# Retention and feed-forward in one kernel: outputs of two chunks in two PSUM banks, first up projections paired, first down projections by rows of w_out, first block's results evicted by ScalarE

## The chip, the cores and the metric

The kernel runs on one core of a Trainium2 chip. The metric is the device time of one execution in microseconds (us); the kernel before has a median of 309.3 us over 3 runs (308.94 to 309.8). Times inside an execution are counted from the start of the profiled span.

The engines are named as the profile names them: PE (TensorE, matrix multiplication; PEld is its weight load), DVE (VectorE), ACT (ScalarE), POOL (GpSimd) and SP (SyncE, which here only issues transfers). Each engine works through its own queue in order; engines wait for each other through semaphores.

## The reference

Eight batches, eight heads, 576 positions, head size 64. A retention layer without softmax feeds a two-layer feed-forward block with a gated activation:

```python
scores = scale * np.matmul(q, k.transpose(0, 1, 3, 2))
gamma = 1.0 - 2.0 ** (-5.0 - np.arange(H))
rel = pos[:, None] - pos[None, :]
Dmat = np.where(rel >= 0, gamma[:, None, None] ** rel[None, :, :], 0.0)
attn = np.matmul(scores * Dmat, v)
x = attn.transpose(0, 2, 1, 3).reshape(B * S, H * D)   # 4608 x 512
h = x @ w_in                                           # 512 -> 2048
g = h * (1.0 / (1.0 + np.exp(-beta * h)))
return g @ w_out                                       # 2048 -> 512
```

All inputs and the output are float32. The kernel multiplies in bfloat16.

## The kernel before, in words

**Blocks and chunks.** The first 512 positions of each batch are one block of 512 rows. The last 64 positions of all eight batches together are a ninth block. A block's attention is worked in four chunks of 128 keys. Index `i` counts chunks over all blocks in the order of `seq`: 0 to 3 are block 0, 4 to 7 block 1, 8 to 11 block 2.

**One chunk.** `pre` casts keys (`kn`) and scales values (`vn`) on POOL. `t_k` transposes the keys on PE into a PSUM tile `T`, and another engine copies it to `kT` (from block 2 on, a DMA transposes instead: `x_q`, `x_k`). `a_sc` makes the scores of all heads in two PSUM tiles, and DVE multiplies them by the causal mask into `R`. `a_cross` adds to the output tile `O` what earlier chunks contribute, from the state `sbd`; `a_O` adds the chunk's own part. `a_x` evicts `O` into `xT`, the transposed input of the feed-forward. `a_st` updates the state in PSUM, and ACT copies it to `sbd` (after a block's last chunk to `end`).

**Feed-forward.** `up(m, fo)` multiplies block `m`'s `xT` by 128 columns of w_in, four matmuls over `ko`; ACT applies the activation into `gT`. `down(m, ms, f0)` multiplies four rows `fo` of `gT` for a 128-row slice `ms` by four row groups of w_out; after the last of sixteen rows the slice is evicted from `po` to `ot` and stored. Block 1's first ten ups run in halves (256 columns), so that they can begin with chunks 4 and 5 alone.

**Weights.** w_in and w_out are loaded once, in float32, through a tile `wt` with four buffers, and cast to bfloat16 in SBUF: w_in in pieces of 256 or 512 columns by `cast_w_in`, w_out in four groups of four row groups by `cast_w_out`, which also divides by beta. Before the change w_in has four pieces of 256 and two of 512 columns, one transfer each. In the 256-column pieces DVE casts `ko` 0 and 1 and POOL 2 and 3; in the larger ones POOL casts only `ko` 3. ACT casts the last row group of each group of w_out.

**PSUM.** Eight banks: the tag `mm` has three (ups, downs, some transposes and scores), `O` two, `sc` two, `st` one. A tile takes a buffer of its tag when the buffer's last reader in program order is done.

**Order.** It is written out by hand. Block 0's attention is a straight list of calls with small matmuls between (`warm_up`), followed by `cast_w_in(0)` and `(1)`. From then on PE follows one list, `fill`: the ups of block 0 (16 entries), its downs (`d0` is their first index, 16 entries), the ups of block 1 (`u1`), and so on. All other work hangs on positions in that list: each entry of `streams` is a pair of a position and a call, and `merged` emits a call just before the first fill entry whose index is at least its position. So `(d0 + 10.6, t_q)` is emitted before fill entry `d0 + 11`. All transfers but one go through the queue of SP, in the order of emission, and move on the same sixteen DMA engines.

Of the kernel before, what the change touches and what calls it, by code (L numbers as in the profile page):

```python
# [19 lines left out]
def kernel(  # L20
# [127 lines left out]
    causal4 = consts.tile([P, HP, P], BF16, name="causal4")  # L148
    nc.gpsimd.tensor_copy(causal4[:], causal[:].unsqueeze(1).to_broadcast([P, HP, P]))

# [16 lines left out]
    pieces = [(f, 256) for f in range(0, 1024, 256)] + [(f, 512) for f in range(1024, d_ff, 512)]  # L167
# [5 lines left out]
    def load_w_in(g):  # L173
        f0, fn = pieces[g]
        if f0 % 512 == 0:
            whole[0] = stage.tile([P, KO, 512], F32, name="wt", tag="wt", bufs=4)
        t = whole[0][:, :, f0 % 512:f0 % 512 + fn]
        nc.sync.dma_start(t, w_in_r[:, :, f0:f0 + fn])  # L178
        wts[g] = t

    def cast_w_in(g, kos=range(KO)):
        t = wts[g]
        f0, fn = pieces[g]
        for ko in kos:
            on_pool = ko == KO - 1 or g < 4 and ko > 1
            (nc.gpsimd if on_pool else nc.vector).tensor_copy(w_in_sb[:, ko, f0:f0 + fn], t[:, ko])  # L186
# [6 lines left out]
    def cast_w_out(g):  # L193
        t = wts.pop(NP + g)
        for i in range(KO):
            fo = g * KO + i
            if i == KO - 1:
                nc.scalar.activation(w_out_sb[:, fo, :], t[:, i], ACT.Copy, scale=rbeta_sb[:, fo:fo + 1])
            else:
                nc.vector.tensor_scalar(w_out_sb[:, fo, :], t[:, i], rbeta_sb[:, fo:fo + 1], None, ALU.mult)  # L200
# [99 lines left out]
    def t_k(i):  # L300
        T = psum.tile([P, HP, P], BF16, name="T", tag="sc" if i in (CB + 2, CB + 3) else "O", bufs=2)
        for p in range(HP):
            nc.tensor.transpose(T[:, p, :], heads(live[i]["kn"], p), ident[:])
        nc.scalar.copy(live[i]["kT"], T[:])  # L304
# [8 lines left out]
    def a_sc(i):  # L313
        L = live[i]
        L["R"] = R = sb.tile([P, 2, HP, P], BF16, name="R", tag="R", bufs=4)

        tag = "mm" if i == CB - 1 else "O" if i >= E and (i - E) % 2 else "sc"
        sc = [psum.tile([P, HP, P], F32, name="sc", tag=tag, bufs=3 if tag == "mm" else 2) for _ in range(2)]
        for p in range(HP):
            for j in range(2):  # L320
                r = slice(j * D, (j + 1) * D)
                rhs, view = q_cols(i, r, p)
                nc.tensor.matmul(view(sc[j][:, p, :]), L["kT"][r, p, :], rhs, start=True, stop=True,  # L323
                                 skip_group_check=True)
        mask = causal if seq[i][0] is not None else causal2
        m_b = mask[:].unsqueeze(1).to_broadcast([P, HP, P])
        if i == CB - 1:

            half = sb.tile([P, HP, P], BF16, name="half", tag="half", bufs=1)
            nc.scalar.copy(half[:], sc[1][:])  # L330
            sc[1] = half
        for j in range(2):
            nc.vector.tensor_tensor(R[:, j], sc[j][:], causal4[:] if i == CB - 1 else m_b, ALU.mult)  # L333

    def a_cross(i, first):

        b, c = seq[i]
        L = live[i]
        if first:
            L["O"] = psum.tile([P, HP, P], F32, name="O", tag="O", bufs=2)  # L340
        if c == 0 and b is not None:
            return
        for p in range(HP):
            rhs, view = q_cols(i, slice(0, P), p)
            if b is None:
                for x in range(2):
                    r = slice(x * TL, (x + 1) * TL)
                    nc.tensor.matmul(L["O"][:, p, r], ends[(2 * c + x) % 4][:, p, :], rhs[:, r],  # L348
                                     start=False, stop=True, skip_group_check=True)
            else:  # L350
                nc.tensor.matmul(view(L["O"][:, p, :]), sbds[(c - 1) % NS][:, p, :], rhs,  # L351
                                 start=first and p == 0, stop=not first, skip_group_check=True)

    def a_O(i):
# [5 lines left out]
        if not early:  # L360
            tag = "sc" if b is not None and b >= QB and c > 1 else "O"
            L["O"] = psum.tile([P, HP, P], F32, name="O", tag=tag, bufs=2)
        O, R, vn = L["O"], L["R"], L["vn"]
        crossed = b is None or c > 0
        for j, p in [(n // HP, n % HP) if early else (n % 2, n // 2) for n in range(H)]:
            nc.tensor.matmul(O[j * D:(j + 1) * D, p, :], vn[:, 2 * p + j, :], R[:, j, p, :],  # L366
                             start=p == 0 and not (early and crossed), stop=early or not crossed,
                             skip_group_check=True)
        if early:
            a_x(i)  # L370

    def a_x(i):
        b, c = seq[i]
        O = live[i]["O"]
        if b is None:
            x = xt(B)[:, :, c, :]
        else:
            x, O = xt(b)[:, :, :, c * PC:(c + 1) * PC], O.rearrange("k p (i s) -> k p i s", i=CB)
        if i == CB - 1:
            nc.vector.tensor_copy(x[:, :2], O[:, :2])  # L380
            nc.scalar.copy(x[:, 2:], O[:, 2:])
        else:
            on_act = i < E or i % 2 == 0 if i < 2 * E else b is not None and c == 1
            (nc.scalar.copy if on_act else nc.vector.tensor_copy)(x, O[:])  # L384
# [31 lines left out]

    pos_, ots, held = {}, {}, []
# [5 lines left out]
    def down(m, ms, f0, fn=4, n0=0, nn=d_model):  # L423
# [13 lines left out]
        nc.vector.tensor_copy(ot, po[:, :nn])  # L437
# [43 lines left out]
    a_O(0)  # L481
    a_sc(1)
# [7 lines left out]
    t_k(3)  # L490
    warm_up(1, 128)
    a_cross(2, True)
    a_sc(3)
    pre(2, (1,))
    a_st(2)
    a_O(2)
    pre(3, (1,))
    warm_up(2, 128)
    a_cross(3, True)
    a_O(3)  # L500
    cast_w_in(0)
# [9 lines left out]
    fill = [F(up, 0, fo) for fo in range(FO)]  # L511
    d0 = len(fill)
    fill += [F(down, 0, ms, f0) for f0 in range(0, FO, 4) for ms in range(3)]
# [14 lines left out]
    def second(i):  # L528
        for f in (a_O, lambda j: a_cross(j, False), a_x):
# [4 lines left out]
    streams = [[(0, F(load_w_out, 0)), (1.1, F(cast_w_in, 2)), (3.1, F(cast_w_in, 3)), (3.2, F(load_w_out, 1)),  # L534
                (6.1, F(cast_w_in, 4)), (6.2, F(load_w_out, 2)), (10.1, F(cast_w_in, 5)), (10.2, F(load_w_out, 3))],
# [6 lines left out]
               [(d0 + 7, F(pre_q, 1, n)) for n in range(4)] + [(d0 + 12.5, F(pre_q, XB, n)) for n in range(4)] + [(d0 + 10.6, F(t_q, 1, 0)), (d0 + 12.6, F(t_q, 1, 1))],  # L542
               [(d0 + 8, F(pre, 4, (0,))), (d0 + 8, F(pre, 5, (0,))), (d0 + 9, F(pre, 4, (1,))), (d0 + 9, F(pre, 5, (1,))),
                (d0 + 12.7, F(t_k, 4)), (d0 + 12.8, F(t_k, 5)), (d0 + 13.8, F(a_sc, 4)), (d0 + 13.81, F(a_sc, 5)),
                (d0 + 14.8, F(a_st, 4)), (d0 + 15.9, F(second, 4))],
               [(d0 + 10, F(pre, 6, (0,))), (d0 + 10, F(pre, 7, (0,))), (d0 + 12, F(pre, 6, (1,))), (d0 + 12, F(pre, 7, (1,))),
                (d0 + 15.8, F(t_k, 6)), (d0 + 15.91, F(t_k, 7)), (u1 + 1.8, F(a_sc, 6)), (u1 + 1.81, F(a_sc, 7)),
                (u1 + 2.8, F(a_st, 6)), (u1 + 8.8, F(second, 6))]]
# [32 lines left out]
    for n in range(1, B - 1):  # L581
# [3 lines left out]
        lo, hi = (base[n] + 16, base[n + 1] - 9.5) if n == 1 else (base[n] + 3, base[n + 1] - 8)  # L585
# [44 lines left out]
```

## Time and profile before

The profiled execution took 309.26 us, of which 307.6 us are the span of the program's instructions. The rest of this text counts in that execution.

| what | us |
|---|---|
| median of 3 runs | 309.3 |
| profiled execution | 309.26 |
| its span | 307.6 |
| PE busy in the span | 297.1 (97%) |
| PE idle | about 10.5 |
| first up of block 0 starts | 19.08 |
| first down of block 0 starts | 34.00 |
| first up of block 1 starts | 52.10 |
| last matmul ends | 303.9 |

The feed-forward's matmuls are most of it: the page gives the up projections (line 413) 128.2 us of PE and the down projections (line 430) 126.5. The transfers are busy early: until 40 us the queue moves 211 to 388 GB/s, and its sixteen engines show busy shares around 1.0 in every stretch. Group lines read as: line, engine, operation, output from inputs with their sizes, count, then busy time and the mean of one. Timeline lines read as: start, length, engine, line, operation, count, and in brackets the engine's idle time before it with what ended that.

### The profile page before, as it was taken

The numbers are of one execution on the slowest core, as the hardware profiler recorded it, in microseconds if no ns is written. First come the engines' busy times: TensorE is split into PE (matmuls) and PEld (weight loads), VectorE is DVE, ScalarE is ACT, GpSimd is POOL, SyncE is SP. The second block draws the span as 40 slices with busy tenths as digits, with TensorE's granted clock in tenths as the row PEclk, the third lists the DMA queues.
The fourth block names the chain that finished last, engine by engine and source line by source line (L and its number), as shares of the span: only waits on it lengthen the run. The fifth ranks groups of instructions, "written<-read, shape, count | busy, mean of one in ns | idle before, by whom it ended". The sixth has DMA issues, their size and how long they took to land.

```text
span 307.6 us, 5289 instructions
## 1 busy us (share of the span) xinstructions
PE 297.1 (97%) x2112; PEld 156.5 (51%) x2145; DVE 106.0 (34%) x190; ACT 141.6 (46%) x251; POOL 96.6 (31%) x131
## 2 busy tenths in 40 slices
PE   8889999999999999999999999999999999999995
PEld 6543456755554454454554545454545544444444
DVE  7554476304730433234430623052424520020012
ACT  5666626882248313660286208710772048107600
POOL 4753016836433392181326030912330000000000
PEclk9999999999999999999999999999999999999999
DMA  8999999999999999997994499939980110121012
GB/s 210 221 357 387 380 238 265 209 187 275 182 268 237 244 219 227 251 169 158 196 245 86 105 226 241 181 90 206 200 125 16 76 49 0 33 69 36 0 68 70
DMA packets 128120, 53.84 MB, mean 175 GB/s; under 512 B 109904, under 2 KB 120544, under 8 KB 128096
## 3 DMA queue, kind: packets, MB, share of 16 engines
q1 hardware_dynamic: 128064, 53.49, 78.3%
q8 instruction: 17, 0.28, 0.4%
q14 instruction: 7, 0.06, 0.1%
q10 hardware_dynamic: 32, 0.01, 0.0%
HBM read 36.71 MB, written 9.44 MB: 150 GB/s over the span
## 4 chain that ended last, share of the span: by engine, by line
PE 88%; SPq 4%; DMA 4%; issue 1%; DVE 1%; ACT 0%
PE po L430 40%; PE ph L413 38%; DMA wt<-in_moe_w_in_dram 4%; SPq L94 3%; PE sc L323 3%; PE O L366 3%; PE st L396 2%; PE O L351 2%; SPq L178 1%; DVE xT L384 0%; DVE w_in_sb L186 0%; PE O L348 0%; SPq L81 0%; PE T L297 0%; ACT sbd L401 0%
## 5 line engine op out<-in xcount | busy, mean ns | idle before, releaser
L415 ACT ACTIVATE gT<-ph,beta_sb 128x512 bf16<-128x512 f32 (+1 forms) x154 | 100.2, 660 | 83.0 <-PE ph L413 82.6
L413 PE MATMUL ph<-xT,w_in_sb 128*128 128x512 bf16 (+1 forms) x600 | 128.2, 365 | 2.6 <-DVE w_in_sb L186 0.9
L430 PE MATMUL po<-w_out_sb,gT 128*128 128x512 bf16 (+2 forms) x591 | 126.5, 368 | 1.0 <-issue 0.3
L413 PEld LDWEIGHTS <-w_in_sb 128*128 128x128 bf16 x616 | 58.9, 98 | 64.8 <-DVE w_in_sb L186 2.5
L430 PEld LDWEIGHTS <-gT 128*128 128x128 bf16 x608 | 57.1, 98 | 62.6
L333 DVE TENSOR_TENSOR R<-sc,causal 128x512 bf16<-128x512 f32 x71 | 44.3, 684 | 78.3 <-PE sc L323 78.3
L437 DVE COPY ot<-po 128x512 f32<-128x512 f32 (+2 forms) x38 | 25.0, 662 | 85.9 <-PE po L430 85.8
L255 POOL TENSOR_TENSOR vn<-kvn,gv 128x512 bf16<-128x512 f32 x32 | 33.3, 1044 | 17.8 <-DMA kvn<-in_v_dram 9.1
L273 POOL CAST kn<-kvn 128x512 bf16<-128x512 f32 x32 | 19.6, 613 | 52.4 <-DMA kvn<-in_k_dram 51.9
L247 POOL TENSOR_TENSOR qs<-qn,gq 128x512 bf16<-128x512 f32 x24 | 24.3, 1043 | 26.4 <-DMA qn<-in_q_dram 26.4
L401 ACT CAST sbd<-st 64x256 bf16<-64x256 f32 x48 | 17.4, 363 | 18.6 <-PE st L396 18.0
L384 DVE CAST xT<-O 128x512 bf16<-128x512 f32 x24 | 15.8, 688 | 18.7 <-PE O L366 9.1
L384 ACT CAST xT<-O 128x512 bf16<-128x512 f32 x11 | 6.5, 587 | 31.4 <-PE O L351 31.2
L396 PE MATMUL st<-vn,kn 128*128 128x128 bf16 x128 | 12.4, 219 | 0.1
L396 PEld LDWEIGHTS <-kn 128*128 128x128 bf16 x128 | 9.2, 98 | 4.8
L366 PE MATMUL O<-R,vn 128*64 128x128 bf16 x288 | 11.2, 221 | 0.1
L366 PEld LDWEIGHTS <-vn 128*64 128x64 bf16 x288 | 8.8, 109 | 4.3 <-issue 3.8
L323 PE MATMUL sc<-qT,kT 64*128 64x128 bf16 x256 | 10.3, 217 | 0.3 <-ACT kT L304 0.2
L262 POOL TENSOR_TENSOR kn<-tln,gq 128x512 bf16<-128x512 f32 x4 | 4.2, 1044 | 18.9 <-DMA tln<-in_q_dram 13.6
L323 PEld LDWEIGHTS <-kT 64*128 64x128 bf16 x288 | 8.1, 94 | 3.6 <-ACT kT L304 1.1
L208 PE MATMUL ph<-warm 128*128 128x128 f32 (+1 forms) x24 | 7.3, 444 | 1.2 <-DVE warm L119 1.2
L186 DVE CAST w_in_sb<-wt 128x256 bf16<-128x256 f32 (+1 forms) x14 | 5.8, 464 | 5.5 <-DMA wt<-in_moe_w_in_dram 5.4
(56 smaller groups left out, 84.8 us busy)
## 6 DMA issues: line engine op xcount, KB each, us to landing
qn<-in_q_dram SPq DMA_DIRECT2D x16, 512.0 KB, 5.7
kvn<-in_k_dram SPq DMA_DIRECT2D x32, 256.0 KB, 4.8
kvn<-in_v_dram SPq DMA_DIRECT2D x32, 256.0 KB, 5.1
out_dram<-ot SPq DMA_DIRECT2D x31, 256.0 KB, 3.1
wt<-in_moe_w_out_dram SPq DMA_DIRECT2D x4, 1024.0 KB, 9.5
wt<-in_moe_w_in_dram SPq DMA_DIRECT2D x4, 512.0 KB, 7.5
wt<-in_moe_w_in_dram SPq DMA_DIRECT2D x2, 1024.0 KB, 11.9
out_dram<-ot SPq DMA_DIRECT2D x9, 128.0 KB, 2.4
```

Source lines behind the costliest of these rows:

```text
L247: e.tensor_tensor(batch[b]["qs"][:, cs, hs], q_tiles[b][:, hs, cs].rearrange("p h i d -> p i h d"), gq[:, cs, hs].unsqueeze(3).to_broadcas ...
L255: nc.gpsimd.tensor_tensor(live[i]["vn"][:], kv_tiles.pop(i)[:, 1], gains(gv, c), ALU.mult)
L273: nc.gpsimd.tensor_copy(kn[:, c % 2], t[:, 0])
L323: nc.tensor.matmul(view(sc[j][:, p, :]), L["kT"][r, p, :], rhs, start=True, stop=True, skip_group_check=True)
L333: nc.vector.tensor_tensor(R[:, j], sc[j][:], causal4[:] if i == CB - 1 else m_b, ALU.mult)
L366: nc.tensor.matmul(O[j * D:(j + 1) * D, p, :], vn[:, 2 * p + j, :], R[:, j, p, :], start=p == 0 and not (early and crossed), stop=early or ...
L384: (nc.scalar.copy if on_act else nc.vector.tensor_copy)(x, O[:])
L396: nc.tensor.matmul(st[:, p, :], heads(L["kn"], p), heads(L["vn"], p), start=(c == 0 and p == 0), stop=True, skip_group_check=True)
L413: nc.tensor.matmul(ph, w_in_sb[:, ko, fo * P:(fo + 1) * P], xts[m][:, ko, :, w], start=(ko == 0), stop=(ko == KO - 1))
L415: nc.scalar.activation(gts[m][:, fo, :, w], ph, ACT.Silu, scale=beta_sb[:, fo:fo + 1])
L430: nc.tensor.matmul(po[:, :nn], gT[:, fo, ms, :], w_out_sb[:, fo, n0:n0 + nn], start=(fo == 0), stop=(fo == FO - 1))
L437: nc.vector.tensor_copy(ot, po[:, :nn])
```

## The change

Its parts, in the order of the program:

1. The mask copy `causal4` is gone; the scores of chunk 3 are masked by DVE straight from both PSUM tiles, without the copy `half` by ACT.
2. w_in has six pieces of 256 columns and one of 512. The first two and the last are loaded in two transfers each (`ko` 0, 1 and `ko` 2, 3). POOL casts `ko` 0 and 1 of piece 0, and `ko` 1 and 3 of the others; the 512-column piece is cast for `ko` 2 and 3 in halves of 256 columns.
3. POOL instead of ACT casts the last row group of w_out's first group.
4. The output tiles of chunks 3 and 5 are split over two PSUM buffers (`split`, `new_O`, `O_of`, `opens`); DVE evicts one, ACT the other.
5. `a_x` is called by itself in the front, for chunk 1 after `t_k(3)`; `a_sc(3)` goes ahead of `a_cross(2)`.
6. Evictions: in block 1 ACT takes chunk 4 whole and half of chunk 5, DVE the rest; DVE copies `kT` of chunks 6 and 7; ACT evicts block 0's downs.
7. The first two ups of block 0 are paired: `ko` 0 and 1 of both, then `ko` 2 and 3 of both. The first twelve down matmuls go row group by row group over three slices.
8. Positions: block 1's and block 2's attention steps are shifted among the fill entries.

```diff
-    causal4 = consts.tile([P, HP, P], BF16, name="causal4")
-    nc.gpsimd.tensor_copy(causal4[:], causal[:].unsqueeze(1).to_broadcast([P, HP, P]))
...
-    pieces = [(f, 256) for f in range(0, 1024, 256)] + [(f, 512) for f in range(1024, d_ff, 512)]
+    pieces = [(f, 256) for f in range(0, 1536, 256)] + [(f, 512) for f in range(1536, d_ff, 512)]
...
-        nc.sync.dma_start(t, w_in_r[:, :, f0:f0 + fn])
+        for w in (slice(0, 2), slice(2, KO)) if g in (0, 1, NP - 1) else (slice(0, KO),):
+            nc.sync.dma_start(t[:, w], w_in_r[:, w, f0:f0 + fn])
...
-            on_pool = ko == KO - 1 or g < 4 and ko > 1
-            (nc.gpsimd if on_pool else nc.vector).tensor_copy(w_in_sb[:, ko, f0:f0 + fn], t[:, ko])
+            on_pool = ko < 2 if g == 0 else ko % 2
+            e = nc.gpsimd if on_pool else nc.vector
+            if fn > 256 and ko == 2:
+                for x in range(0, fn, 256):
+                    for o, eng in ((2, nc.vector), (3, nc.gpsimd)):
+                        eng.tensor_copy(w_in_sb[:, o, f0 + x:f0 + x + 256], t[:, o, x:x + 256])
+            elif fn == 256 or ko < 2:
+                e.tensor_copy(w_in_sb[:, ko, f0:f0 + fn], t[:, ko])
...
-            if i == KO - 1:
+            if i == KO - 1 and g == 0:
+                nc.gpsimd.tensor_tensor(w_out_sb[:, fo, :], t[:, i], rbeta_sb[:, fo:fo + 1].to_broadcast([P, d_model]), ALU.mult)
+            elif i == KO - 1:
...
-        nc.scalar.copy(live[i]["kT"], T[:])
+        (nc.vector.tensor_copy if i in (CB + 2, CB + 3) else nc.scalar.copy)(live[i]["kT"], T[:])
...
-        if i == CB - 1:
-
-            half = sb.tile([P, HP, P], BF16, name="half", tag="half", bufs=1)
-            nc.scalar.copy(half[:], sc[1][:])
-            sc[1] = half
...
+    def split(i):
+        return i in (CB - 1, CB + 1)
+
+    def new_O(i):
+        b, c = seq[i]
+        if split(i):
+            tags = ("sc", "sc") if i == CB - 1 else ("O", "sc")
+            live[i]["O"] = [psum.tile([P, 2, P], F32, name="O", tag=t, bufs=2) for t in tags]
+        else:
+            tag = "sc" if b is not None and b >= QB and c > 1 else "O"
+            live[i]["O"] = [psum.tile([P, HP, P], F32, name="O", tag=tag, bufs=2)]
...
-        if i == CB - 1:
-            nc.vector.tensor_copy(x[:, :2], O[:, :2])
-            nc.scalar.copy(x[:, 2:], O[:, 2:])
+        if split(i):
+            nc.vector.tensor_copy(x[:, :2], view(Os[0]))
+            nc.scalar.copy(x[:, 2:], view(Os[1]))
         else:
-            on_act = i < E or i % 2 == 0 if i < 2 * E else b is not None and c == 1
+            on_act = i < E + 2 or i >= 2 * E and b is not None and c == 1
...
+    def up_pair(m, fo, u):
...
+        fs = (fo, fo + 1)
+        if u == 0:
+            for f in fs:
+                phs[f] = psum.tile([P, MB], F32, name="ph", tag="mm", bufs=3)
+        for f, ko in [(f, ko) for ko in (0, 1) for f in fs] if u == 0 else [(f, ko) for f in fs for ko in (2, 3)]:
+            nc.tensor.matmul(phs[f][:], w_in_sb[:, ko, f * P:(f + 1) * P], xts[m][:, ko],
+                             start=(ko == 0), stop=(ko == KO - 1))
+            if ko == KO - 1:
+                nc.scalar.activation(gts[m][:, f], phs[f][:], ACT.Silu, scale=beta_sb[:, f:f + 1])
...
-        nc.vector.tensor_copy(ot, po[:, :nn])
+        (nc.scalar.copy if m == 0 else nc.vector.tensor_copy)(ot, po[:, :nn])
...
-    a_cross(2, True)
-    a_sc(3)
+    a_x(1)
+    warm_up(1, 128)
+    a_sc(3)
+    a_cross(2, True)
...
-    fill = [F(up, 0, fo) for fo in range(FO)]
+    fill = [F(up_pair, 0, fo, u) for fo in (0,) for u in range(2)] + [F(up, 0, fo) for fo in range(2, FO)]
     d0 = len(fill)
-    fill += [F(down, 0, ms, f0) for f0 in range(0, FO, 4) for ms in range(3)]
+    def down_rows(n):
+
+        for x in range(4 * n, 4 * n + 4):
+            down(0, x % 3, x // 3, 1)
+
+    fill += [F(down_rows, n) for n in range(3)]
+    fill += [F(down, 0, ms, f0) for f0 in range(4, FO, 4) for ms in range(3)]
     fill += [F(down, 0, 3, f0) for f0 in range(0, FO, 4)]
```

The positions that change, by call (others stay):

| call | before | after |
|---|---|---|
| `t_q(1, 0)` | d0 + 10.6 | d0 + 11.6 |
| `t_k(5)` | d0 + 12.8 | d0 + 14 |
| `a_sc(4)`, `a_sc(5)` | d0 + 13.8, 13.81 | d0 + 14, 15 |
| `a_st(4)` | d0 + 14.8 | d0 + 15 |
| `t_k(6)`, `t_k(7)` | d0 + 15.8, 15.91 | d0 + 15.95, u1 + 1 |
| `a_sc(6)`, `a_sc(7)` | u1 + 1.8, 1.81 | u1 + 2, 3 |
| `a_st(6)`, `second(6)` | u1 + 2.8, 8.8 | u1 + 4, 8 |
| `first(8)`, `first(10)` | base[1] + 16, base[2] - 9.5 | base[1] + 17, base[2] - 7.5 |

`second(i)` gives the outputs of chunks `i` and `i + 1`; `first(i)` their scores. The loads of w_out and the casts of w_in's pieces follow the pieces to new positions among block 0's ups.

## The prediction

> **What bounds the kernel now.** I read the page first (which engine, and whether the stall is spread or local), then PE's waits and timeline, then the timeline of all engines around each stall.
>
> ```profile
> span 307.6 us, 5289 instructions
> PE 297.1 (97%) x2112; PEld 156.5 (51%) x2145; DVE 106.0 (34%) x190; ACT 141.6 (46%) x251; POOL 96.6 (31%) x131
> ```
>
> PE is the bound, and the change removes no matmul. Only idle time of PE can be won, and all of it that this change can reach lies before 60 us: PE's timeline shows no wait on another engine from 60 us to the last matmul at 303.9.
>
> ```profile
> 18.15 0.40 PE L396 MATMUL st<-vn,kn 128*128 128x128 bf16 x4
> 19.08 0.39 PE L413 MATMUL ph<-xT,w_in_sb 128*128 128x512 bf16 x1 [0.53 <-DVE w_in_sb L186]
> 19.70 7.12 PE L413 MATMUL ph<-xT,w_in_sb 128*128 128x512 bf16 x31 [0.24 <-POOL w_in_sb L186]
> 27.18 6.98 PE L413 MATMUL ph<-xT,w_in_sb 128*128 128x512 bf16 x30 [0.36 <-DVE w_in_sb L186]
> 34.00 2.32 PE L430 MATMUL po<-w_out_sb,gT 128*128 128x512 bf16 x10
> ```
>
> Columns: start, length, engine, line, operation, count, idle before it and who ended it. A 512-column matmul starts every 0.2158 us when nothing waits (19.70 to 19.92 to the next). The 64 of block 0's up projection need 13.81 us; they take from 19.08 to 34.00, 14.92. So 1.11 us are stalls: 0.41 at 19.08 (second matmul), 0.70 around 26.4 to 27.5. Counted back from 34.00, the ups run as if they had started at 20.19.
>
> ```profile
> 18.27 0.42 DVE L380 CAST xT<-O 128x256 bf16<-128x256 f32 x1 [1.04 <-PE O L366]
> 18.73 0.69 DVE L186 CAST w_in_sb<-wt 128x256 bf16<-128x256 f32 x2
> 18.73 0.37 ACT L381 CAST xT<-O 128x256 bf16<-128x256 f32 x1 [0.71 <-DVE xT L380]
> 18.76 0.92 POOL L186 CAST w_in_sb<-wt 128x256 bf16<-128x256 f32 x2 [1.93 <-DMA wt<-in_moe_w_in_dram]
> 25.95 1.51 DVE L186 CAST w_in_sb<-wt 128x512 bf16<-128x512 f32 x3 [2.02 <-DMA wt<-in_moe_w_in_dram]
> 25.98 0.87 POOL L186 CAST w_in_sb<-wt 128x512 bf16<-128x512 f32 x1 [1.79 <-DMA wt<-in_moe_w_in_dram]
> ```
>
> Two things end together at 18.7: the outputs of chunk 3 (ACT's half waits for DVE's half of the same bank) and w_in's first piece. The casts of the 512-column piece then stop PE at 26 to 27.5.
>
> The transfers behind this come one after another on a full queue. Landings in the trace: w_in 18.70, 20.21, 21.70, 23.20 (512 KB each), 25.92, 28.63 (1024 KB); w_out 31.33, 34.05, 36.74, 39.45; block 1's q 40.94 and 42.53, then k and v every 1.1. Of the first piece's sixteen completions fifteen arrive at 16.85 to 17.20 and the last at 18.70: a 16 KB instruction packet ran from 16.37 for 1.15 us, and one DMA engine stays 1.5 us behind the rest until 36.
>
> **Part 1: the front.** Chunk 3's chain. ACT no longer copies `half` (0.59) nor takes xT of chunk 1 (0.59) before kT of chunk 3, so kT(3) runs 14.72 to 15.31 instead of 15.06 to 15.65, and the scores of chunk 3 go at 15.36. DVE masks both halves from PSUM, 1.29 as its row for chunk 2, 15.87 to 17.16 (before: ready 17.23). st(2) comes at 15.9, ACT's copies of it (0.76) end at 17.1 instead of 17.41, and the cross term and outputs of chunk 3 end at 17.75 instead of 18.2. With two banks DVE (0.42) and ACT (0.37) evict side by side: x ready at 18.25, not 19.10. The removed `causal4` copy (0.61 on POOL at 3.08) lies before a wait of 2.70 on POOL (for beta, line 218) and is worth nothing.
>
> w_in. Piece 0's first half needs half the packets and ends about 0.75 before its second, at 16.2, ahead of the instruction packet. POOL is busy with vn until 16.83, then casts its two rows (0.92) by 17.8. The paired ups use these rows for four matmuls from 18.3 to 19.17; the second half (18.70, cast by DVE to 19.08 and 19.42) is then 0.1 late. After that each piece is checked at 0.35 (DVE) or 0.46 (POOL) per cast and 0.05 for the semaphore: piece 1's second half 20.2, first needed 20.56: 0.1 late. Piece 2 lands 21.70, cast 22.08, needed 21.95: 0.18 late. Piece 3 23.20 against 23.86, piece 4 (now 256 columns) 24.7 against 25.6, piece 5 26.2 against 27.3, piece 6's halves 27.6 and 28.9 against 29.06 and 29.5: all in time. So the ups run as from 18.68, bound by piece 2, and end at 32.49: 1.51 earlier. If no straggler forms, from 18.35.
>
> Price: two pieces of 512 KB took 2 x 1.50 where one of 1024 KB took 2.71, so all later landings move by 0.3. Four more transfers are issued on SP. Their own cost is bounded by nothing below (the packets of a 512 KB piece alone fill its 1.50) and, above, by the 128 KB tail transfers, which land every 0.65 where 256 KB of k or v with the same 256-byte rows takes 1.2: 0.1 each. The w_in row is the nearer one, so I take nothing: w_out lands 0.3 late, at most 0.7.
>
> The Trainium skill speaks against this part ("DMA: Bandwidth & Descriptors", section Bandwidth): transfers should be gathered to at least 1 MiB, and its section on the anatomy of a DMA puts a fixed cost of about 2.0 us on each. By that, exposed, four more would cost 8 us. This queue's spacing of 1.50 and 2.71 shows no such term, because the completions overlap.
>
> **Part 2: the first downs.** `down_rows` touches three PSUM banks in its first three matmuls, where the old order opened one every four. They are the banks of ups 13, 14 and 15, so the third matmul waits for the last SiLU.
>
> ```profile
> 34.20 0.69 ACT L415 ACTIVATE gT<-ph,beta_sb 128x512 bf16<-128x512 f32 x1 [0.18 <-PE ph L413]
> 49.17 1.03 PE L430 MATMUL po<-w_out_sb,gT 128*128 128x512 bf16 x4
> 50.35 0.68 DVE L437 COPY ot<-po 128x512 f32<-128x512 f32 x1
> 50.99 0.59 ACT L384 CAST xT<-O 128x512 bf16<-128x512 f32 x1
> 51.35 0.69 DVE L384 CAST xT<-O 128x512 bf16<-128x512 f32 x1 [0.32 <-PE O L351]
> 52.10 1.05 PE L413 MATMUL ph<-xT,w_in_sb 128*128 128x256 bf16 x8 [0.34 <-DVE xT L384]
> 55.95 1.47 PE L413 MATMUL ph<-xT,w_in_sb 128*128 128x256 bf16 x12 [0.17 <-ACT gT L415]
> 58.58 0.69 DVE L384 CAST xT<-O 128x512 bf16<-128x512 f32 x1 [2.58 <-PE O L351]
> ```
>
> The last SiLU ends 0.89 after the ups do (34.89 against 34.00); the third matmul wants to start after 0.43: **a new wait of 0.48**. All later downs queue behind it on PE. It hides one thing: w_out's fourth group, landing 39.45 plus 0.3, and its casts (rows of 0.48 on DVE, 0.40 apart, the third matmul needing the third row) allow its downs at landing + 0.94 = 40.7. PE alone would be there at 32.49 + 0.48 + 36 x 0.2158 = 40.74; before it was 41.77. So **1.03 is kept**, and without the new wait w_out would have taken most of the 0.48 anyway. Row 3 of group 0 goes to POOL (0.87 as its copy, 1.04 as its product): from 31.8 to 32.9, needed at 34.4. Its ACT cast (0.72) that stood between SiLUs goes; PE never waited for it.
>
> **Part 3: block 1 under the downs.** ACT evicts block 0's downs: no such row; 0.59 (its copy to bf16) to 0.72 (its scaled copy), I take 0.59. kT of chunks 6 and 7 goes to DVE (qT there: 0.69 for twice the size, so 0.37 to 0.69). t_q(1,0) moves back one down (0.86), needing qs at 42.75 and due at 43.4. Before the first up of block 1, ACT now does ot (0.59), x of chunk 4 (0.59) and half of chunk 5 (0.37) in a row: up at 1.82 after the last down. Before, the down of 49.17 gave PE free at 50.03, DVE took its ot, and the up came at 52.10: 2.07 with a transposition of 0.22 that now comes later: 0.03 gained. The wait at 52.10 thus stays. Among the half ups the stall at 55.95 (0.34) comes from ACT's 0.76 copy of the state in front of the SiLUs; a_st(6), one up later, leaves 0.27. Both x of chunks 6 and 7 on DVE end 0.46 later, with one more half up (0.43) as cover: 0.28 against 0.29. Some 0.12 gained, between -0.3 and 0.5.
>
> Block 2: scores of chunks 10 and 11 go two downs later; its kT lands at 75.71, used at 76.35 before, and at 76.9 against 76.2 after. outputs(8) then keeps two downs (1.73) as cover for three DVE copies of 0.69 that need 1.0 of it. Nothing there.
>
> Sum: -1.03 - 0.03 - 0.12 = -1.18 on the profiled execution's 309.26 (span 307.56 plus 1.70 around it, unchanged), which equals the median of 309.3: **308.1**.
>
> **Rivals.**
> *A, the straggler does not bite* (0.17): the packet comes with PE's program, at about the same matmul, but may hit between pieces. Ups as from 18.35, w_out earlier: 0.35 more, 307.8; with the stalls of part 3 gone too (0.27 + 0.28) 307.2. The Trainium skill ("Runtime: NRT & Kernel Launch", Instruction fetch mechanics) calls a 16 KiB refill mostly hidden; the row of 1.15 us and the late sixteenth completion say that here it is not, for the transfers.
> *B, the gain is eaten by the exchange of waits* (0.25): transfers at 0.1 each put w_out's downs at 41.1, and ACT's ot at 0.72 lengthens block 1's first wait by 0.13, its stalls by 0.3: 0.67 - 0.1 - 0.3 = 0.3 to 0.7 kept, 308.8.
> *C, slower* (0.08): the halves of w_in run at the pace of k and v, 256 KB in 1.20. The four halves of pieces 0 and 1 then take 0.45 more each (1.8), the two of piece 6 2.40 instead of 1.36 (2.1). The last group of w_out lands at 39.45 + 0.3 + 1.8 + 2.1 = 43.65 and its downs start at 44.6 instead of 41.77: 2.8 lost, 0.1 regained, 312.0. It turns the sign once w_out's last landing passes 40.83. Against it: the packets are still 1 and 2 KB, and those of 1 KB moved at 350 GB/s, the 256-byte ones of k and v at 217.
>
> **Chances and range.** Forecast 0.50, A 0.17, B 0.25, C 0.08. 0.3% of 309.3 is 0.93 us, about what can be told from no change. The forecast (own range 307.6 to 308.6) lies just beyond 308.4: 0.45 of its 0.50 faster. With A and a small part of B: faster 0.64; same 0.29; slower 0.07. Range 307.2 (A with part 3) to 309.1 (B's upper end).
>
> **What would show it.** First up near 18.4 and the first down near 32.5; a PE gap of some 0.5 at the third down, ended by ACT gT; w_out's last landing near 39.8; the first up of block 1 near 50.9 still behind an xT copy; no PE wait on another engine after 59. Wrong if the ups start after 19.0, if PE waits on w_out casts from 35 to 42, or if scores of block 2 wait for their transposed keys.

## The result and the profile after

The changed kernel takes **308.39 us** (median of 20 runs, 307.78 to 309.35), the kernel before beside it 309.32 (20 runs, 308.62 to 311.13). The ratio is 0.9967, with a 95% interval of 0.9955 to 0.9978: faster by 0.7 to 1.4 us. The forecast was 308.1, range 307.2 to 309.1.

The profiled execution took 308.57 us. These are the page's first lines:

```profile
span 306.7 us, 5306 instructions
PE 296.6 (97%) x2113; PEld 155.6 (51%) x2145; DVE 105.1 (34%) x190; ACT 141.8 (46%) x251; POOL 99.1 (32%) x136
```

PE is still busy for 97% of the span. By the two pages its busy time fell by 0.5 and its idle time by 0.3 to 0.4, although no matmul was taken out; the ends of matmuls are modelled, so that split isn't to be relied on. Where the time went shows when the starts of the same work are set side by side. The first two columns come from PE's timelines; the last is the prediction's working, cut at the same places.

| from ... to ... | before | after | difference | predicted |
|---|---|---|---|---|
| span's start, first down of block 0 | 34.00 | 32.74 | -1.26 | -1.51 |
| first down, last matmul of block 0's downs | 15.82 | 16.54 | +0.72 | +0.48 |
| that matmul, first half up of block 1 | 2.28 | 1.71 | -0.57 | -0.25 |
| first half up, first whole up of block 1 | 11.60 | 12.10 | +0.50 | +0.10 |
| first whole up, block 2's first up | 23.00 | 23.20 | +0.20 | 0 |
| block 2's first up, last matmul's start | 217.03 | 217.02 | -0.01 | 0 |
| last matmul's start, end of the span | 3.83 | 3.42 | -0.41 | 0 |
| sum | 307.56 | 306.73 | -0.83 | -1.18 |

(A transposition of 0.22 moves from the third row to the fourth.) Five stages up to the last matmul move, and they exchange waits as much as they remove them. The time around the span went from 1.70 to 1.84 in these two executions, where the forecast had it unchanged. Single executions differ among themselves by 1.6 us (after) and 2.5 us (before), so the profile gives the stages, and the medians the time.

PE's timeline of the changed kernel, in the columns of the one before:

```profile
18.61 1.67 PE L445 MATMUL ph<-xT,w_in_sb 128*128 128x512 bf16 x6 [0.28 <-DVE xT L397]
...
20.33 12.57 PE L430 MATMUL ph<-xT,w_in_sb 128*128 128x512 bf16 x55
32.74 0.59 PE L463 MATMUL po<-w_out_sb,gT 128*128 128x512 bf16 x2
33.68 0.59 PE L463 MATMUL po<-w_out_sb,gT 128*128 128x512 bf16 x2 [0.34 <-ACT gT L432]
```

The 55 matmuls of the row at 20.33 run in 12.57 us: two short waits of 0.12 and 0.20 are left among them, and the stall of 0.70 near 27 is gone. The third down then waits for ACT's last `gT`. From the second down's start to the third is 0.72 where 0.216 is its pace: a wait of 0.51.

All engines of the same kernel around the first up:

```profile
16.80 0.74 POOL L190 CAST w_in_sb<-wt 128x256 bf16<-128x256 f32 x2
...
18.04 0.42 DVE L397 CAST xT<-O 128x256 bf16<-128x256 f32 x1 [0.87 <-PE O L385]
18.08 0.37 ACT L398 CAST xT<-O 128x256 bf16<-128x256 f32 x1 [0.28 <-PE O L385]
...
18.97 0.50 DVE L190 CAST w_in_sb<-wt 128x256 bf16<-128x256 f32 x2 [0.51 <-DMA wt<-in_moe_w_in_dram]
```

The two halves of chunk 3's output leave their two banks side by side, and POOL is done with the first half piece by 17.54. The second half still lands late, at 18.95, and DVE casts it then.

All engines around block 1's first ups, and PE's weight loads at block 2's scores:

```profile
48.63 1.03 PE L463 MATMUL po<-w_out_sb,gT 128*128 128x512 bf16 x4
...
49.70 0.59 ACT L470 COPY ot<-po 128x512 f32<-128x512 f32 x1
50.18 0.59 ACT L401 CAST xT<-O 128x512 bf16<-128x512 f32 x1
50.51 0.42 DVE L397 CAST xT<-O 128x256 bf16<-128x256 f32 x1 [0.72 <-PE O L371]
50.66 0.39 ACT L398 CAST xT<-O 128x256 bf16<-128x256 f32 x1
50.99 0.61 PE L430 MATMUL ph<-xT,w_in_sb 128*128 128x256 bf16 x4
...
55.84 0.60 PE L430 MATMUL ph<-xT,w_in_sb 128*128 128x256 bf16 x4 [0.17 <-ACT gT L432]
```

```profile
77.66 0.45 PEld L329 LDWEIGHTS <-kT 64*128 64x128 bf16 x16 [0.30 <-DMA kT<-kn]
```

ACT's three copies start 0.48 apart although the first two are shown with 0.59 each; PE follows 0.33 after the last has begun. The wait behind `gT` at 55.84 is as long as before. The last line is new: scores of block 2 wait for their transposed keys.

### The profile page after: what moved, and what is told of

Same layout as the page of the kernel before. It is cut to its first block, busy times and chain, and to the rows that moved or that the text cites. A ratio compares the mean times of both kernels' runs of the same rounds, so it can differ in the third digit from the quotient of the medians.

```text
span 306.7 us, 5306 instructions
## 1 busy us (share of the span) xinstructions
PE 296.6 (97%) x2113; PEld 155.6 (51%) x2145; DVE 105.1 (34%) x190; ACT 141.8 (46%) x251; POOL 99.1 (32%) x136
## 4 chain that ended last, share of the span: by engine, by line
PE 90%; DMA 4%; SPq 2%; issue 1%; ACT 1%; DVE 1%; POOL 1%
PE ph L430 40%; PE po L463 38%; PE sc L329 3%; PE O L385 3%; DMA kT<-kn 2%; PE O L371 2%; PE st L413 2%; DMA kvn<-in_k_dram 2%; SPq L94 2%; PE ph L445 1%; PE T L309 1%; ACT gT L432 0%; ACT kT L310 0%; PE O L368 0%; POOL vn L261 0%
## 5 line engine op out<-in xcount | busy, mean ns | idle before, releaser
L432 ACT ACTIVATE gT<-ph,beta_sb 128x512 bf16<-128x512 f32 (+1 forms) x152 | 99.1, 659 | 80.7 <-PE ph L430 80.2
L430 PE MATMUL ph<-xT,w_in_sb 128*128 128x512 bf16 (+1 forms) x594 | 126.6, 365 | 0.9 <-ACT gT L432 0.2
L430 PEld LDWEIGHTS <-w_in_sb 128*128 128x128 bf16 x608 | 58.1, 98 | 62.2 <-DVE w_in_sb L190 0.9
L334 DVE TENSOR_TENSOR R<-sc,causal 128x512 bf16<-128x512 f32 x72 | 44.9, 683 | 76.3 <-PE sc L329 76.2
L470 DVE COPY ot<-po 128x512 f32<-128x512 f32 (+2 forms) x34 | 22.4, 659 | 84.8 <-PE po L463 84.8
L190 POOL CAST w_in_sb<-wt 128x256 bf16<-128x256 f32 (+1 forms) x13 | 6.4, 510 | 4.9 <-DMA wt<-in_moe_w_in_dram 4.9
```

The lines of the kernel that those rows point to most:

```text
L334: nc.vector.tensor_tensor(R[:, j], sc[j][:], m_b, ALU.mult)
L430: nc.tensor.matmul(ph, w_in_sb[:, ko, fo * P:(fo + 1) * P], xts[m][:, ko, :, w], start=(ko == 0), stop=(ko == KO - 1))
L432: nc.scalar.activation(gts[m][:, fo, :, w], ph, ACT.Silu, scale=beta_sb[:, fo:fo + 1])
L470: (nc.scalar.copy if m == 0 else nc.vector.tensor_copy)(ot, po[:, :nn])
```

## The experiments

Each time below stands beside runs of the kernel before on the same chip, whose median was 309.31 to 309.39. The profiled execution of a kernel lies up to 0.8 us from its median, so the stages of two kernels may be compared one by one, but not their ends. Unless another kernel is named, edits are to the changed kernel. The diffs show the lines that matter.

**The change once more**, as a control.

> The change itself once more, for comparison with the next three on the same chip. Ratio to the kernel before 0.996 to 0.998. If the engine that fetches PE's instructions is what holds w_in, the last completion of piece 0's first half comes near 16.6, that of its second half 1.2 to 1.5 us after the other fifteen, and the first down near 32.5 to 32.8.

308.44 us, ratio 0.9964 (0.9949 to 0.998). First down at 32.59, w_in's halves at 16.68 and 18.49, the same wait of 0.51 at the third down. The last completion of the second half came 1.09 behind the other fifteen, a little less than the 1.2 to 1.5 expected. The waits at w_in's pieces 1 and 2 are absent here, as those pieces landed 0.5 earlier. The scores of block 2 waited 0.57 this time. So stages repeat to 0.2, but for that one.

**The front alone.** Weights, block 0's attention, paired ups and downs by rows stay; evictions and positions of blocks 1 and 2 are as before.

```diff
-        return i in (CB - 1, CB + 1)
+        return i == CB - 1
...
-        (nc.scalar.copy if m == 0 else nc.vector.tensor_copy)(ot, po[:, :nn])
+        nc.vector.tensor_copy(ot, po[:, :nn])
...
-        lo, hi = (base[n] + 17, base[n + 1] - 7.5) if n == 1 else (base[n] + 3, base[n + 1] - 8)
+        lo, hi = (base[n] + 16, base[n + 1] - 9.5) if n == 1 else (base[n] + 3, base[n + 1] - 8)
```

> The front, the pieces of w_in and the first downs of the change, with block 1's and block 2's steps and evictions as before. Theory (block 1's steps are what lets the front's gain through): first down still near 32.7, but q of block 1 lands no earlier, so t_q(1,0) at d0 + 10.6 waits for its scaled queries and PE loses 0.4 to 0.9 us between 41 and 46; time 308.8 to 309.2, and the first half up of block 1 near 51.7. Rival (the front's gain goes through by itself): no wait there, first half up near 51.3 with both transpositions done, time 308.3 or less.

309.77 us, 1.0009 (0.9993 to 1.0026). The first down is at 32.92, 1.08 earlier than before, yet the first half up is at 52.08, where it was before. The lead goes in two waits: 0.51 at the third down, and 0.56 after the down of 44.01, where the next waits for DVE's `ot`:

```profile
44.05 1.88 DVE L470 COPY ot<-po 128x512 f32<-128x512 f32 x3
...
44.79 1.02 PE L463 MATMUL po<-w_out_sb,gT 128*128 128x512 bf16 x4 [0.39 <-DVE ot L470]
```

The expectation had put a wait of that size at block 1's `qT`; it is at the eviction. The half up and the median are later than expected, by 0.4 and 0.6.

**Block 1 alone.** The front as before; positions, evictions and the split of chunk 5 as in the change.

```diff
-    fill = [F(up_pair, 0, fo, u) for fo in (0,) for u in range(2)] + [F(up, 0, fo) for fo in range(2, FO)]
+    fill = [F(up, 0, fo) for fo in range(FO)]
...
-    fill += [F(down_rows, n) for n in range(3)]
-    fill += [F(down, 0, ms, f0) for f0 in range(4, FO, 4) for ms in range(3)]
+    fill += [F(down, 0, ms, f0) for f0 in range(0, FO, 4) for ms in range(3)]
```

> The front as before, block 1's and block 2's steps and evictions of the change. First down at 34.0. Theory: the step from the last down to the first half up is 0.3 shorter, but the scores of chunks 4 to 7, now one by one, cost 0.2 more per pair, so by 63 us nothing is gained: 309.2 to 309.5. Rival (the two parts add up): 308.9, the step's 0.3 stays in the time.

309.26 us, 0.9993 (0.9976 to 1.0009). First down to last down group takes 16.04 (before 15.82), that group to the half up 1.71 (2.28), half up to whole up 12.11 (11.60): block 1's part wins 0.57 and gives 0.22 and 0.51 back. **Neither half of the change shows a gain by itself.**

**DVE evicts block 0's downs again**, all else as changed.

```diff
-        (nc.scalar.copy if m == 0 else nc.vector.tensor_copy)(ot, po[:, :nn])
+        nc.vector.tensor_copy(ot, po[:, :nn])
```

> The change with block 0's downs evicted by DVE again. Theory (DVE is busy with block 1's queries when the first three slices end): the fourth slice's first down waits 0.4 to 0.6 for a PSUM bank, ended by DVE's ot; x of chunk 4 goes earlier on ACT, which gives back 0.1 at most; time 308.7 to 309.0. Rival (no matter who evicts): no such wait, 308.4.

309.53 us, 1.001 (0.9998 to 1.0023): the whole gain is gone, 1.1 against the control. The band expected was 308.7 to 309.0. Its timeline (all engines):

```profile
42.94 1.29 DVE L253 TENSOR_TENSOR qs<-qn,gq 128x512 bf16<-128x512 f32 x2 [0.28 <-DMA qn<-in_q_dram]
...
44.15 1.88 DVE L470 COPY ot<-po 128x512 f32<-128x512 f32 x3
...
44.88 0.81 PE L463 MATMUL po<-w_out_sb,gT 128*128 128x512 bf16 x3 [0.56 <-DVE ot L470]
```

Block 1's q lands when the queue has brought it, however early the downs are, and DVE scales it until 44.2. With the downs a microsecond earlier their evictions fall due behind it, and the down that needs the bank waits. First to last down takes 17.26 instead of 16.53, which is this wait, 0.73 from start to start. It accounts for two thirds of the 1.1; this execution, 309.13, was among the fastest of its kernel, and the rest stays open.

In the kernel before, the same two pieces of DVE's work follow each other as well, but no matmul of PE waits for the evictions there:

```profile
42.56 1.29 DVE L247 TENSOR_TENSOR qs<-qn,gq 128x512 bf16<-128x512 f32 x2 [0.30 <-DMA qn<-in_q_dram]
...
43.77 1.93 DVE L437 COPY ot<-po 128x512 f32<-128x512 f32 x3
```

**The same edit the other way: the kernel before with ACT evicting block 0's downs.**

> The kernel before with one edit: ACT evicts block 0's downs to ot. Theory (the eviction's engine is worth its 0.9 only once the front is earlier, because DVE's scaling of q then falls due beside the evictions; in the kernel before no PE wait hangs on ot, and the first up of block 1 waits for x of chunk 5, which DVE starts when PE's outputs are there, not when ot is done): 309.1 to 309.5, first half up at 52.0 to 52.2. Rival (the eviction on ACT is worth most of the gain by itself, wherever it stands): 308.4 to 308.7, first half up at 51.2 to 51.7.

309.65 us, 1.0002 (0.9989 to 1.0016). Its timeline:

```profile
50.71 0.59 ACT L437 COPY ot<-po 128x512 f32<-128x512 f32 x1
...
51.83 0.69 DVE L384 CAST xT<-O 128x512 bf16<-128x512 f32 x1 [0.92 <-PE O L351]
...
52.58 1.05 PE L413 MATMUL ph<-xT,w_in_sb 128*128 128x256 bf16 x8 [0.34 <-DVE xT L384]
```

DVE, relieved of `ot`, stands idle for 0.92 for PE's outputs of chunk 5, and the half up comes behind the same `xT`. The execution was 0.49 late from its first up on, so the half up misses the band expected; from first up to half up it is 33.01, before 33.02. The time is 0.15 above the band. An exchange of engines worth 1.1 in the medians beside an early front shows no gain beside a late one. Whether the front with this eviction alone, at the old positions, would do as well as the whole change was not run.

**Whole transfers for w_in's pieces 0, 1 and the last.**

```diff
-        for w in (slice(0, 2), slice(2, KO)) if g in (0, 1, NP - 1) else (slice(0, KO),):
+        for w in (slice(0, 2), slice(2, KO)) if False else (slice(0, KO),):
```

> The change with pieces 0, 1 and 6 of w_in in one transfer each. Theory (the halves give the early start): piece 0 lands near 18.8 as a whole, its POOL casts end 0.5 later, the first up starts at 19.3 to 19.5 instead of 18.6, the first down 0.5 to 0.6 later than with halves; but w_out's landings do not move, so the downs catch up part of it: time 0.1 to 0.5 above the change. Rival (piece 2 sets the start anyway): first down within 0.15 of the change's, same time.

308.79 us, 0.9983 (0.9968 to 0.9998). All engines around the first up:

```profile
19.30 0.69 DVE L190 CAST w_in_sb<-wt 128x256 bf16<-128x256 f32 x2 [0.40 <-DMA wt<-in_moe_w_in_dram]
19.33 0.93 POOL L190 CAST w_in_sb<-wt 128x256 bf16<-128x256 f32 x2 [1.98 <-DMA wt<-in_moe_w_in_dram]
...
19.91 1.47 PE L445 MATMUL ph<-xT,w_in_sb 128*128 128x512 bf16 x5 [1.14 <-POOL w_in_sb L190]
```

`xT` is ready at 18.9, but the piece lands whole at 19.28, and PE's idle 1.14 ends with POOL's casts. The first down is at 33.73, 1.14 behind the control where 0.5 to 0.6 were expected; 0.4 of it is there already when `xT` is ready. The halves are worth 0.35 in the medians (308.79 against 308.44, with intervals that overlap); this profiled execution, 309.40, was among the longest of its kernel. Where nothing disturbs them (the longer program, below), halves land 0.75 apart and whole pieces here 1.50: no cost of a transfer shows on this queue.

**The pieces of w_in as before** (four of 256 columns, two of 512), with the halves and the cut casts kept.

```diff
-    pieces = [(f, 256) for f in range(0, 1536, 256)] + [(f, 512) for f in range(1536, d_ff, 512)]
+    pieces = [(f, 256) for f in range(0, 1024, 256)] + [(f, 512) for f in range(1024, d_ff, 512)]
...
-                (4.1, F(cast_w_in, 4)), (6.1, F(cast_w_in, 5)), (6.2, F(load_w_out, 2)), (8.1, F(cast_w_in, 6)),
+                (4.1, F(cast_w_in, 4)), (4.2, F(load_w_out, 2)), (8.1, F(cast_w_in, 5)),
```

> The change with w_in again in four pieces of 256 and two of 512 columns; piece 0, piece 1 and the last are still loaded in two transfers each, and the 512-column casts of ko 2 and 3 stay cut in two. Theory (the small pieces are what removes the stall of 0.70 that the kernel before had near 26 to 27.5 us): a stall of 0.4 to 0.9 behind a w_in cast returns between 25 and 28, the first down starts at 33.1 to 33.5 instead of 32.6 to 32.74, w_out's last group lands 0.2 to 0.3 earlier than in the change; 308.8 to 309.2. Rival (the halves of the casts are enough, or w_out's landing sets the end of the downs anyway): the first down stays within 0.2 of the change, or it is late and the last down of block 0 is not; 308.1 to 308.5.

309.45 us, 0.9996 (0.9983 to 1.001). PE waits 0.25 behind DVE's cast and 0.25 behind POOL's. PE's weight loads:

```profile
26.15 0.10 PEld L430 LDWEIGHTS <-w_in_sb 128*128 128x128 bf16 x1 [0.58 <-DVE w_in_sb L190]
...
26.62 0.24 PEld L430 LDWEIGHTS <-w_in_sb 128*128 128x128 bf16 x2 [0.38 <-POOL w_in_sb L190]
```

The first down is at 33.33, as the theory had it; the half up is 0.74 later than in the control. The time is 0.25 above the theory's band, and w_out's last group landed no earlier than in the control (39.84 against 39.86). The smaller pieces are needed for the gain.

**First downs in the old order of slices.**

```diff
-    fill += [F(down_rows, n) for n in range(3)]
+    fill += [F(down, 0, ms, 0) for ms in range(3)]
```

> The change with block 0's first downs slice by slice again (four rows of one slice at a time). The wait of 0.51 at the third down goes. Theory (it covered a wait that comes anyway): PE now waits for casts of w_out's rows 1 to 3 instead, the 37th down starts within 0.15 of the change's, time 308.3 to 308.6. Rival (the wait costs its full length): 37th down 0.4 to 0.5 earlier, time 307.9 to 308.1.

308.55 us, 0.9966 (0.9952 to 0.9981): as the control. No wait at the third down for `gT`; a wait of 0.18 for a cast of w_out stands there, and first to last down takes 16.25 instead of 16.53. The 37th down is at 40.68, 0.34 before the change's and 0.19 before the control's: between what the theory and the rival wanted. The three edits together, below, show why that isn't a sure gain.

**Scores of chunks 6 and 7 at one position.**

```diff
-                (d0 + 15.95, F(t_k, 6)), (u1 + 1, F(t_k, 7)), (u1 + 2, F(a_sc, 6)), (u1 + 3, F(a_sc, 7)),
+                (d0 + 15.95, F(t_k, 6)), (u1 + 1, F(t_k, 7)), (u1 + 2, F(a_sc, 6)), (u1 + 2, F(a_sc, 7)),
```

> The change with the scores of chunks 6 and 7 side by side again (chunk 7's moved forward by one half up). Theory (each group of scores among other matmuls costs PE 0.1 before and 0.1 after): the way from the first half up to the first whole up is 0.2 shorter than the change's 12.1, minus up to 0.1 if chunk 7's transposed keys come late. Rival (these gaps are an artefact of modelled ends): same length within 0.05. The time, 308.2 to 308.4, can hardly tell.

308.61 us, 0.9968 (0.9949 to 0.9987). Half up to whole up takes 11.89 instead of 12.10. PE loses 0.1 going into a group of 64-row scores and 0.1 coming out of it, so two groups apart cost 0.21 more than two in a row. In the total it can't be seen: w_in's first half landed at 18.40 in this execution, and the scores of block 2 waited 0.31; the median is 0.2 above the band.

**Block 2's scores one down later**, with the outputs behind them kept in place.

```diff
-        lo, hi = (base[n] + 17, base[n + 1] - 7.5) if n == 1 else (base[n] + 3, base[n + 1] - 8)
+        lo, hi = (base[n] + 17, base[n + 1] - 6.5) if n == 1 else (base[n] + 3, base[n + 1] - 8)
...
-                st.append((t + 5, F(outputs, i - 2)))
+                st.append((t + (4 if n == 1 else 5), F(outputs, i - 2)))
```

> The change with the scores of chunks 10 and 11 one more down later, their outputs where they were. Theory (the transposed keys of block 2's second half now land too late, and PE waits 0.2 to 0.6 for them): that wait goes, nothing takes its place, PE's last matmul 0.2 to 0.6 earlier, time 308.0 to 308.2. Rival (the wait is only in the profiled executions, or DVE's masks become the next one): 308.4 or more.

308.29 us, 0.9962 (0.9949 to 0.9976). Whole up to block 2's first up is 23.00 again, but the keys landed at 76.22 here, and would have been in time without the edit: inconclusive by itself.

**The last three edits together.**

> The change with three edits: first downs in the old order of slices, scores of chunks 6 and 7 at one position again, first(10) one down later. Theory (each edit removes one wait that was seen in another kernel, and the waits lie at places that don't share a cover): first down to last down of block 0 is 16.25 instead of 16.53 (as in the run with the slices alone), first half up to first whole up of block 1 is 11.89 instead of 12.10 (as in the run with the paired scores), and block 1's first whole up to block 2's first up is 23.00 with no wait for kT. Together 0.5 to 0.9 off the control: 307.5 to 307.9. Rival (the row-wise order and the slices are equal, because w_out's last group or the queue of DVE sets the downs' end; the last edits' gain is returned before block 2): 308.2 to 308.5.

308.18 us, 0.9963 (0.9945 to 0.998): the fastest median, short of the theory's band, and not to be told from the control. All engines at the first downs:

```profile
31.73 2.06 DVE L206 TENSOR_SCALAR w_out_sb<-wt,rbeta_sb 128x512 bf16<-128x512 f32 x3 [2.08 <-DMA wt<-in_moe_w_out_dram]
31.78 1.33 POOL L202 TENSOR_TENSOR w_out_sb<-wt,rbeta_sb 128x512 bf16<-128x512 f32 x1 [1.87 <-DMA wt<-in_moe_w_out_dram]
...
33.45 1.42 PE L463 MATMUL po<-w_out_sb,gT 128*128 128x512 bf16 x5 [0.38 <-DVE w_out_sb L206]
```

w_out's first group landed at 31.63, in the run with the slices alone 0.5 earlier. The slices want its rows in four matmuls, and two waits of 0.54 and 0.18 came for them: 16.75 from first to last down. By rows the wait is 0.51 whatever the landing (31.06 to 32.21 in the runs here); by slices it is 0.18 to 0.72. The landing is not all of it: DVE's second row, which ran beside POOL's product, took 1.26 instead of 0.48. An estimate from these rows: at the 1.28 that DVE's three rows take without POOL the third would have been ready at 33.01, and the third matmul, due at 33.12, would not have waited. Slices with ACT's old cast of the fourth row were not run. The theory's sum fails there. Its two other terms hold: 11.90 and 22.99. The keys landed at 77.74 and PE used them at 78.28; one down (0.86) earlier it would have waited 0.3.

**A longer PE program ahead of block 0.** 40 short matmuls in place of three longer ones, whose results are not read.

```diff
-    warm_up(5)
+    warm_up(2)
+    for _ in range(8):
+        warm_up(5, 4)
```

> The change with 38 short matmuls more among the first dummy ones on PE, whose results nobody reads; PE's instruction list is then longer by some 40 entries ahead of the attention of block 0. Theory (PE's 16 KB packet of instructions comes when PE has worked through a given number of them, and whichever w_in transfer it meets on its DMA engine lands 1.1 to 1.7 late): the packet of 15.7 to 15.9 comes some 1.0 to 1.7 earlier, and the first half of w_in's piece 0 lands at 17.5 or later instead of 16.6 to 16.8, with the first up at 18.9 or later. Rival (the late completion belongs to the second half's place in the queue, not to the packet): the first half lands at 16.5 to 16.9 whatever the packet does, and the second at 18.5 to 18.9.

322.15 us (2 runs). The short matmuls were not short: 80 records in some 17 us, 0.2 each at 4 columns, so all of PE came some 14 us later and the packet at 20.99 instead of earlier. The question is answered all the same. With no packet at 16, the two halves of piece 0 land at 16.76 and 17.51, those of piece 1 at 18.23 and 18.97: 0.75 apart, none late; the next two, around the packet, take 2.09 and 2.16 instead of 1.50. In the changed kernel and its control the packet came at 15.89 and 15.68, and the second half landed at 18.95 and 18.49. The rival (the place in the queue) wanted 18.5 to 18.9. The packet can hit the first half instead: it came at 16.15 in the kernel with paired scores, whose first half landed at 18.40 and whose first up came at 19.04. Which half it hits does not follow from its time alone, and the delay, 1.1 to 1.7, is not quite the packet's own 1.1 to 1.4.

## Why the prediction came out as it did

The sign and the mechanisms of the front were right; the time was 0.3 above the forecast and inside the range, where it was kept in part by luck. By its steps:

**The front: mechanism right, 0.25 too much.** Two banks let `xT` go at 18.46, where 18.25 was expected, and the first up followed at 18.61 (18.3). The first half piece landed untouched by the packet at 16.57 (16.2 expected). The second half was late at 18.95 without costing anything, and the waits at pieces 1 and 2 came as predicted: 0.12 and 0.20 against 0.1 and 0.18. In the control they did not come, and the ups run without a stall from their start at 18.78. The first down came at 32.74 (32.59 in the control) instead of 32.49. Without the small pieces the median is 1.0 above the control's, without the halves 0.35. Two banks for chunk 3 and the pairing of the first ups were not tested alone. w_out's last group landed at 40.00, 0.55 later than before, where the prediction took 0.3 and allowed 0.7.

**The new wait at the third down: right**, 0.51 against 0.48. Its justification, that w_out's fourth group would have taken most of it anyway, was not tested: no run shows PE waiting for that group. By the prediction's own 0.94 behind the landing, the slices of the first edit alone could have had it at 40.19 and came at 40.68. What takes the wait's place there is the first group, 0.18 to 0.72. What went wrong beside it: while POOL multiplied its row of w_out (1.33, priced at 1.04 as its other products), DVE's three rows took 2.06 instead of 1.28. By rows it lay under the wait for `gT`.

**"1.03 is kept": 0.54.** Of the missing 0.49 the first down accounts for 0.25. The rest is the 0.22 for standing the scores of chunks 4 and 5 apart; block 1 alone shows it too, 16.04 against 15.82. The step counted instructions and their durations, and these were unchanged; a change of neighbours has its own price.

**"0.03 gained" before block 1's first up: too cautious by 0.32.** It measured 0.35 (2.28 to 1.71, less the 0.22 of the transposition). The prediction's sum 0.59 + 0.59 + 0.37 had ACT's copies one behind the other; they start 0.48 apart. The Trainium skill ("Perfetto Trace Analysis", section Optimizing Scalar/DVE Operations) says that an instruction's profiled latency is longer than the time the engine is taken, because the acknowledgement of its write overlaps with the next one. The rows at 49.70, 50.18 and 50.66 agree: 0.48 from start to start where 0.59 is shown.

**"Some 0.12 gained" among the half ups: 0.28 lost** (0.50 less 0.22). The stall behind the state's copy stayed at 0.336 instead of 0.27, the one behind `xT` went to 0.22 to 0.23 (0.28 predicted), and the scores of chunks 6 and 7 standing apart took 0.21. The prediction overlooked one more: after the first score of chunk 6 at 52.19 PE starts the next 0.15 later, when DVE's second copy of `kT` is done, 0.14 more than such a pair takes otherwise. With the transposition these make up the 0.50. In size this is the largest miss of a stage, 0.40.

**"Block 2: nothing there": wrong in 3 of the 9 profiled executions that keep these positions**, the changed kernel's among them; such a wait was one of the prediction's own signs of being wrong. It moved the landing of the keys from 75.71 to 76.2 and left 0.7 of cover before 76.9. They landed at 77.62, and between 75.33 and 77.84 in the kernels run here (the longer program left out). Why that moves isn't settled: a late half of block 2's q goes with it in three runs, but in the three edits together that q was in time and the keys were late. SP's issue of their transposition took 3.5 to 4.9 us, whether the keys were late or not; but it began at 70.4 to 71.9 in the four executions with late keys and at 69.4 to 70.1 in the others, but for the late execution with whole transfers. Part of the lateness is thus there before the transfer.

**ACT's eviction of block 0's downs** was priced as a cost of 0.59 on ACT and at nothing on DVE. It is what lets the front through: without it a wait of 0.73 comes at 44.1. The prediction had asked which engine would be late, and not what DVE would have to do at the new time of the downs.

The errors are 0.25, 0.24, 0.40 and 0.20 too hopeful and 0.32 too cautious, 0.77 in all. The stages up to the last matmul thus gave 0.41 of the 1.18 in the profiled execution, and another 0.41 came at the end of the span, of which no step spoke. That the total stayed near the forecast is luck in this part. 0.35 of it lies in POOL's closing instructions: its last drain follows the instruction before it after 0.35 in the kernel before and after 0.03 in the changed one. The two other kernels with the old front pause alike, and in these three an instruction packet of 8 KB stands 0.29 behind the span's end, which those with the new front don't have there. That the packet and the pause belong together was not tested. Nor is it shown that the end is a gain in the medians: the front alone has the short end as well, and its median is no lower than before.

**The rivals.** A (no late completion) had the right cause, and the experiment with the longer program shows what it would look like; in the changed kernel it did not happen. B (waits exchanged) described what happened, but with other places: 0.72 (0.48 of it forecast), 0.28 and 0.20 given back. C fell: the halves of w_in move at the pace of the whole.

## What to carry to other kernels

A front that starts earlier moves everything behind it against the landings, which here did not move with it; look at each engine's queue at the new time, above all at evictions behind work that a transfer releases. Try the parts alone and together: here neither half alone showed a gain, and one eviction's engine was worth 1.1 us or nothing that shows, depending on what stood beside it. When a wait is moved, ask how it depends on a landing: a fixed 0.51 and one between 0.18 and 0.72 gave medians that can't be told apart.

## What the runs showed of the hardware

- **Instruction packets delay data.** One packet of 16 KB, of PE's instructions by its size and number, took 1.0 to 1.4 us beside busy queues, and one completion of sixteen came late with it: 18.95 for a half whose other fifteen were in by 17.30. The transfer counts as landed only with the last. The Trainium skill ("Runtime: NRT & Kernel Launch", Instruction fetch mechanics) calls this refill mostly hidden; for PE's own instructions no run here contradicts it, but for a transfer that is waited for these landings do.
- **Short groups cost at their borders.** 64-row scores between full matmuls took 0.1 going in and 0.1 coming out, for 8 of them as for 16.
- **DVE and POOL slow each other.** Three scaled copies of w_out on DVE took 2.06 beside one product on POOL and 1.28 in the next three groups without it; the one that ran under the product took 1.26, the other two 0.49 and 0.47. POOL's product took 1.33 instead of 1.04.
- **A matmul of 4 columns in float32 isn't free:** some 0.2 us a record.
